# One core: convolution steps traced between matmul groups, 512-column weight blocks, tables behind the layer norm, small outputs in one store

## The chip, the cores and the metric

The kernel runs on one core of a Trainium2 chip. The metric is device time in microseconds (us): the median of three runs of the whole kernel. A profiled execution beside them gives the rows quoted here; its span is the time from its first to its last instruction.

## The reference

Two branches work on the layer norm of `A_q` and their outputs are added to it; the kernel computes the output and nine gradients, one for each differentiable input.

```python
def _A_ref(q, k, v, shift_k, ssm_k, ssm_D):          # S = 2048, D = 1024
    k_shift = sum(k_pad[:, t:t + S, :] * shift_k[:, ks - 1 - t] for t in range(ks))   # ks = 4 taps
    kv = k_shift * v
    y = irfft(rfft(kv, 2 * S) * rfft(ssm_k, 2 * S), 2 * S)[:S]      # long convolution per channel
    return q * (y + kv * ssm_D)

def _B_ref(x, W_gate, W_up, W_down):                 # F = 3584
    gate, up = x @ W_gate, x @ W_up
    return ((gate * (gate > 0)) * up) @ W_down

xn = layernorm(A_q)
out = A_q + _A_ref(xn, A_k, A_v, A_shift_k, A_ssm_k, A_ssm_D) + _B_ref(xn, B_W_gate, B_W_up, B_W_down)
# and the gradients of all ten inputs but B_x for grad_out
```

(The sums are written shorter here than in the original.)

## The kernel before

Everything is traced into one Tile program. A list scheduler orders each engine's instructions from the trace: among those that it estimates to be ready it takes the lowest rank, `tc.cur_priority`, which a helper class `Pri` sets. The queues of the engines are then fixed and in order; SyncE (SP) issues every DMA.

**The layer norm** (`layer_norm`, L465) takes 16 row tiles in batches of 1, 1, 2, 4, 4 and 4: two passes of ScalarE (ACT) per tile with an accumulated sum (L478, L485), a root per batch (L489), scalings on VectorE (DVE), a store of the normed rows to `xn_d`, and 8 transposes on TensorE (PE) into `xnT`. It has rank -10,000,000.

**The convolution branch** (`ABranch`) works on 8 groups of 128 channels with a table-driven Fourier transform of 8192 points, split into two matmul steps with a transposition (`flip`, two 32x32 stream transposes on VectorE) between them. `tables` (L101) computes the sine tables on ACT and VectorE. `loads` (L226) brings a group's six input tiles. `group` (L366) then runs in one go: the taps' row (`shift_b`), the transposed filter (`h_tile`), three forward transforms (`forward`: 8 matmuls of 512 columns, four ACT copies, `flip`, 32 matmuls of 128 columns, copies), the four taps on `k` (`taps`, L259, VectorE), three products of spectra (`cmul`), three inverse transforms (`inverse`, then `to_time` with 8 matmuls of 512 columns or `to_chan` with 32 of 64 columns), the gradients of `v`, `k` and of the taps (16 matmuls of 512 columns, `ps6`), and stores. The tap gradient `gsb` is stored element by element (4 x 128 values, L412), the gradient of `ssm_D` as one column of `ghn` (L421). Its matmuls and loads have rank 0 and up, its copies, VectorE work and stores 20,000,000 and up.

**The matmul branch** (`LnMlp`), rank 10,000,000 and up, has six stages: gate and up (`gate_up`, L511), hidden gradient (`grad_hidden`, L539), the gradient of the down weight (`grad_down`, L587), those of the gate and up weights (`grad_in`, L604), the output (`out_phase`, L636) and the input gradient (`grad_x`, L669). The first four walk the 3584 columns in 14 blocks of 256. `gate_up` writes the relu'd gate `rg`, the masked `up` and their product `ht` to DRAM; `grad_hidden` loads `rg` and `up` again, multiplies both with the hidden gradient and stores `gg_d` and `gu_d`. The pools: 16 row tiles (`act`) that hold in turn `xnT`, `goT`, `g_nat` and `xn_nat`; 5 weight blocks; 9 eviction tiles of 128 KB; 4 PSUM banks beside the 4 of the convolution.

So two rank ranges decide the order of the work: a convolution matmul goes ahead of any stage matmul as soon as the scheduler thinks it ready, and a convolution copy goes behind any eviction of the stages. The output stage needs the convolution's result `y_d`.

Of the kernel before, what the change touches and what calls it, by code (L numbers as in the profile page):

```python
# [11 lines left out]
BF16 = mybir.dt.bfloat16  # L12
F32 = mybir.dt.float32
# [4 lines left out]
P = 128  # L18
# [3 lines left out]
class Pri:  # L22


    def __init__(self, tc):
        self.tc = tc
        self.n = 0

    def at(self, base):
        self.n += 1  # L30
        self.tc.cur_priority = base + self.n


PR_LN = -10_000_000
PR_A_PE = 0
PR_A_LD = 0
PR_B = 10_000_000
PR_A_EV = 20_000_000
# [3 lines left out]
class ABranch:  # L42
# [18 lines left out]
    def mm(self, out, lhsT, rhs, start=True, stop=True):  # L61
        self.pri.at(PR_A_PE)
        self.nc.tensor.matmul(out, lhsT=lhsT, rhs=rhs, start=start, stop=stop)  # L63

    def act(self, out, in_):
        self.pri.at(PR_A_EV)
        self.nc.scalar.copy(out=out, in_=in_)

    def tt(self, out, in0, in1, op):
        self.pri.at(PR_A_EV)  # L70
        self.nc.vector.tensor_tensor(out=out, in0=in0, in1=in1, op=op)  # L71

    def vcopy(self, out, in_):
        self.pri.at(PR_A_EV)
        self.nc.vector.tensor_copy(out=out, in_=in_)

    def load(self, out, in_):
        self.pri.at(PR_A_LD)
        self.nc.sync.dma_start(out=out, in_=in_)

    def store(self, out, in_):
        self.pri.at(PR_A_EV)
        self.nc.sync.dma_start(out=out, in_=in_)

    def open(self):
        R = "right"
        self.con = self.pool("a_con", 1, side=R)
        self.lng = self.pool("a_lng", 2, side=R)
# [4 lines left out]
        self.tmp = self.pool("a_tmp", 2, side=R)  # L93
        self.sm = self.pool("a_sm", 2, side=R)
# [6 lines left out]
    def tables(self):  # L101
        nc, con, big, pri = self.nc, self.con, self.big, self.pri
        pri.at(PR_A_LD)
# [11 lines left out]
        self.skf = con.tile([P, self.NG, 4], F32, name="skf")  # L115
        negpi = con.tile([P, 1], F32, name="negpi")
# [109 lines left out]
    def loads(self, gi):  # L226
        nc, pri = self.nc, self.pri
        cg = slice(gi * P, (gi + 1) * P)
        S = self.S
        hn = self.ld.tile([P, 16, P], BF16, name="hn")  # L230
        self.load(hn[:].rearrange("p r c -> p (r c)"), self.ssm_k[cg, :])
        kp = self.lng.tile([P, 19, P], BF16, name="kp")
        pri.at(PR_A_LD)
# [6 lines left out]
        gt = self.ld.tile([P, 16, P], BF16, name="gt")  # L240
        self.load(gt[:], self.tview(self.g, cg))
        xt = self.ld.tile([P, 16, P], BF16, name="xt")
        self.load(xt[:], self.tview(self.xn_d, cg))
        return dict(gi=gi, cg=cg, hn=hn, kp=kp, vt=vt, gt=gt, xt=xt)

    def shift_b(self, st):
        gi = st["gi"]
        dg = self.sm.tile([P, 4, P], BF16, name="dg", bufs=1)
        for i in range(4):
            self.pri.at(PR_A_EV)  # L250
# [8 lines left out]
    def taps(self, st, out, src, offs):  # L259

        skb = st["skb"]
        for n, (i, off) in enumerate(offs):
            for hf in range(2):
                rows = slice(off + 8 * hf, off + 8 * hf + 8)
                sb = skb[:, i, :, :].to_broadcast([P, 8, P])
                o = out[:, 8 * hf:8 * hf + 8, :]
                if n == 0:
                    self.tt(o, src[:, rows, :], sb, ALU.mult)
                else:
                    t = self.tmp.tile([P, 16, P], BF16, name="tap", tag="tmp")  # L270
                    self.tt(t[:, 0:8, :], src[:, rows, :], sb, ALU.mult)
                    self.tt(o, o, t[:, 0:8, :], ALU.add)

    def h_tile(self, st):
# [4 lines left out]
        for r in range(16):  # L279
            self.pri.at(PR_A_PE)  # L280
# [4 lines left out]
    def flip(self, src):  # L285
# [4 lines left out]
        for c0 in range(0, 64, 32):  # L290
            self.pri.at(PR_A_EV)
# [3 lines left out]
    def forward(self, src, form_name, add_D=None):  # L295
# [10 lines left out]
        Bf = self.flip(B)  # L306
# [32 lines left out]
    def inverse(self, Q):  # L339
# [8 lines left out]
    def to_time(self, Cf, dst):  # L348
# [9 lines left out]
    def to_chan(self, Cf, dst):  # L358
# [7 lines left out]
    def group(self, st, nxt):  # L366
        nc, pri, gi, cg = self.nc, self.pri, st["gi"], st["cg"]
        kp, vt, gt, xt = st["kp"], st["vt"], st["gt"], st["xt"]
        self.shift_b(st)
        hT = self.h_tile(st)  # L370
        H = self.forward(hT, "H", add_D=self.sDb[:, cg].rearrange("p (o c) -> p o c", o=1))
        ksh = self.lng.tile([P, 16, P], BF16, name="ksh", bufs=1)
        self.taps(st, ksh, kp, [(3, 0), (2, 1), (1, 2), (0, 3)])
        kvt = self.ttile("kvt")
        self.tt(kvt[:, 0:16, :], ksh[:], vt[:], ALU.mult)
        K = self.forward(kvt, "K")
        self.tt(gt[:], gt[:], xt[:], ALU.mult)
        G = self.forward(gt, "G")
        if nxt is not None:
            st["next"] = self.loads(nxt)  # L380
        Y = self.cmul(H, K, False, "Y")
        GKV = self.cmul(H, G, True, "GKV")
        GH = self.cmul(K, G, True, "GH")

        yt = self.ttile("yt")
        self.to_time(self.inverse(Y), yt)
        self.store(self.tview(self.y_d, cg), yt[:, 0:16, :])

        gkv = self.ttile("gkv")
        self.to_time(self.inverse(GKV), gkv)  # L390
# [5 lines left out]
        pri.at(PR_A_EV)  # L396
        nc.gpsimd.memset(gks[:, 16:19, :], 0.0)
        self.store(gks[0:P - 1, 16:19, :], gks[1:P, 0:3, :])
        ps = self.ps.tile([P, 1024], F32, name="ps6", tag="aps")
        for i in range(4):  # L400
            pr = self.tmp.tile([P, 16, P], BF16, name="pr", tag="tmp")
            self.tt(pr[:], gks[:, 0:16, :], kp[:, 3 - i:19 - i, :], ALU.mult)
            for j in range(4):
                self.mm(ps[:, 0:512], self.hsel[:, i, :], pr[:, 4 * j:4 * j + 4, :].rearrange("p r c -> p (r c)"),
                        start=(i == 0 and j == 0), stop=(i == 3 and j == 3))
        gsf = self.sm.tile([4, P], F32, name="gsf", bufs=1)
        pri.at(PR_A_EV)
# [402 lines left out]
```

## Time and profile before

| | us |
|---|---|
| median of 3 runs | 2509.51 |
| lowest and highest run | 2496.64, 2514.35 |
| the profiled execution | 2500.66 |
| its span | 2498.9 |
| TensorE busy in the span | 2073.8 (83%) |
| VectorE busy | 1090.4 (44%) |
| ScalarE busy | 734.7 (29%) |
| GpSimd busy | 10.1 (0%) |

The busy shares are means over stages with different limits. The stages follow one another on TensorE: layer norm to about 62 us, gate and up from 81.7 to about 796, hidden gradient to about 1213, down weight to 1505.5, gate and up weights from there to 1904, output to 2103, input gradient to the end. The convolution lies beside the stages from gate and up to the down weight. A busy TensorE may still run at half speed: the granted clock of a stretch tells how much of it ran at 2.4 GHz (1.00) and how much at 1.2 GHz (0.50).

### The profile page before, as it was taken

How to read it: one execution, taken by the hardware profiler on the slowest of the kernel's cores; microseconds unless marked ns; L12 is line 12 of the kernel's file. 1: busy time of each engine (PE TensorE's matmuls, PEld its weight loads, DVE VectorE, ACT ScalarE, POOL GpSimd, SP SyncE). 2: the span in 40 equal slices, each digit the busy share in tenths (PEclk: the TensorE clock that was granted, in tenths of full speed). 3: DMA queues.
4: the chain of work that ended last, by engine and by line, in shares of the span. 5: the costliest groups of instructions: out<-in, count | busy, mean ns of one | idle time of the engine just before them, and what ended most of it. 6: DMA issues, size and time to landing. Idle time of an engine off the chain costs nothing. (4 is left out here: it accounts for less than half of the span.)

```text
span 2498.9 us, 36518 instructions
## 1 busy us (share of the span) xinstructions
PE 2073.8 (83%) x14931; PEld 1413.2 (57%) x15050; DVE 1090.4 (44%) x1778; ACT 734.7 (29%) x889; POOL 10.1 (0%) x30
## 2 busy tenths in 40 slices
PE   2784977868588657756778989999999999999998
PEld 1563756757466545544544437888886444444443
DVE  7784866868578257636757300000000221323323
ACT  9633545345363325335455311111110000000000
POOL 0000000000000000000000000000000000000000
PEclk9897989989899888988889999999999999999999
DMA  7347354463638787777852875343436995544542
GB/s 217 101 130 76 115 112 122 131 109 102 117 104 189 200 147 187 200 155 166 234 86 84 169 241 169 106 123 106 121 106 147 262 220 128 136 108 124 119 114 70
DMA packets 749993, 353.18 MB, mean 141 GB/s; under 512 B 422665, under 2 KB 721665, under 8 KB 749826
## 3 DMA queue, kind: packets, MB, share of 16 engines
q1 hardware_dynamic: 749826, 350.85, 58.4%
q8 instruction: 117, 1.92, 0.4%
q14 instruction: 50, 0.41, 0.1%
HBM read 154.93 MB, written 124.79 MB: 112 GB/s over the span
## 5 line engine op out<-in xcount | busy, mean ns | idle before, releaser
L525 PEld LDWEIGHTS <-xnT 128*128 128x128 bf16 x3584 | 351.9, 99 | 76.5 <-issue 23.8
L615 PEld LDWEIGHTS <-xn_nat 128*128 128x128 bf16 x3584 | 350.3, 98 | 48.7 <-DMA xn_nat<-xn_d 7.6
L559 PE MATMUL ps_h<-wdT,goT 128*128 128x256 bf16 x1792 | 227.9, 287 | 51.7 <-ACT gh L562 51.6
L664 DVE TENSOR_TENSOR o<-ps_o,ya 128x512 bf16<-128x512 f32 x32 | 21.4, 687 | 528.1 <-PE ps_o L662 528.1
L525 PE MATMUL ps_g<-wg,xnT 128*128 128x256 bf16 x1792 | 233.3, 277 | 0.1
L525 PE MATMUL ps_u<-wu,xnT 128*128 128x256 bf16 x1792 | 231.0, 276 | 0.2
L559 PEld LDWEIGHTS <-goT 128*128 128x128 bf16 x1792 | 182.6, 103 | 77.4 <-issue 45.6
L596 PE MATMUL ps_d<-g_nat,hs 128*128 128x512 bf16 x870 | 206.5, 389 | 19.2 <-DMA hs<-h_d 12.6
L615 PE MATMUL ps_w<-ggs,xn_nat 128*128 128x256 bf16 x1792 | 201.4, 274 | 4.1 <-DMA xn_nat<-xn_d 3.5
L662 PE MATMUL ps_o<-wd,hT 128*128 128x512 bf16 x878 | 194.6, 381 | 4.7 <-DMA hT<-h_d 3.7
L693 PE MATMUL ps_x<-wgT,ggT 128*128 128x512 bf16 x879 | 197.6, 379 | 0.9
L693 PE MATMUL ps_x<-wuT,guT 128*128 128x512 bf16 x877 | 197.3, 379 | 0.9
L615 PE MATMUL ps_w<-gus,xn_nat 128*128 128x256 bf16 x1792 | 197.9, 273 | 0.0
L618 ACT CAST wi<-ps_w 128x512 bf16<-128x512 f32 x112 | 65.5, 585 | 333.2 <-PE ps_w L615 333.2
L596 PEld LDWEIGHTS <-hs 128*128 128x128 bf16 x896 | 87.8, 100 | 125.1 <-issue 17.0
L662 PEld LDWEIGHTS <-hT 128*128 128x128 bf16 x896 | 87.8, 98 | 111.1 <-DMA hT<-h_d 5.0
L693 PEld LDWEIGHTS <-ggT 128*128 128x128 bf16 x896 | 87.6, 98 | 105.8
L693 PEld LDWEIGHTS <-guT 128*128 128x128 bf16 x896 | 87.6, 98 | 105.7
L63 PE MATMUL ps<-flp,FW 128*128 128x128 bf16 x768 | 58.7, 228 | 82.1 <-DVE flp L292 51.8
L562 ACT CAST gh<-ps_h 128x512 bf16<-128x512 f32 x112 | 66.1, 596 | 191.5 <-DMA gg_d<-upl 98.8
L695 DVE CUSTOM_DVE_ANT_0 gx<-ps_x,gy 128x512 f32<-128x512 f32 x32 | 22.1, 691 | 225.4 <-PE ps_x L693 214.7
L530 ACT ACTIVATE rg<-ps_g 128x512 bf16<-128x512 f32 x112 | 67.7, 605 | 170.3 <-PE ps_g L525 99.0
(165 smaller groups left out, 2110.9 us busy)
## 6 DMA issues: line engine op xcount, KB each, us to landing
rg_d<-rg SPq DMA_DIRECT2D x112, 128.0 KB
up_d<-up SPq DMA_DIRECT2D x112, 128.0 KB
h_d<-ht SPq DMA_DIRECT2D x112, 128.0 KB
rgl<-rg_d SPq DMA_DIRECT2D x112, 128.0 KB
upl<-up_d SPq DMA_DIRECT2D x112, 128.0 KB
gg_d<-upl SPq DMA_DIRECT2D x112, 128.0 KB
gu_d<-gh SPq DMA_DIRECT2D x112, 128.0 KB
hs<-h_d SPq DMA_DIRECT2D x28, 512.0 KB
```

What stands on the lines that cost most here:

```text
L63: self.nc.tensor.matmul(out, lhsT=lhsT, rhs=rhs, start=start, stop=stop)
L525: nc.tensor.matmul(ps[:, s * 256:s * 256 + 256], lhsT=xT[:, kt * P:(kt + 1) * P], rhs=w[:, kt, :], start=(kt == 0), stop=(kt == self.DT - 1))
L530: nc.scalar.activation(out=fl(rg), in_=pss[0][:], func=ACT.Relu)
L559: nc.tensor.matmul(ps[:, s * 256:s * 256 + 256], lhsT=xT[:, kt * P:(kt + 1) * P], rhs=w[:, kt, :], start=(kt == 0), stop=(kt == self.DT - 1))
L562: nc.scalar.copy(out=fl(gh), in_=ps[:])
L596: nc.tensor.matmul(ps[:], lhsT=hs(st)[:, j * P:(j + 1) * P], rhs=gn[st][:, ob * 512:ob * 512 + 512], start=(st == 0), stop=(st == self.ST ...
L615: nc.tensor.matmul(ps[:, d * 256:d * 256 + 256], lhsT=xn[st][:, dc * P:(dc + 1) * P], rhs=sl(st), start=(st == 0), stop=(st == self.ST - 1))
L618: nc.scalar.copy(out=wo[:].rearrange("p s f -> p (s f)"), in_=ps[:])
L662: nc.tensor.matmul(ps[:], lhsT=hT[:, kt, :], rhs=self.wd[:, kt, oc], start=(kt == 0), stop=(kt == self.FT - 1))
L664: nc.vector.tensor_tensor(out=o0[:, oc], in0=ps[:], in1=ya[:, oc], op=ALU.add)
L693: nc.tensor.matmul(ps[:], lhsT=T[:, kt, :], rhs=W[:, kt, oc], start=(i == 0), stop=(i == n - 1))
L695: V.tensor_tensor_reduce(out=gx[:, oc], in0=ps[:], in1=gy[:, oc], scale=1.0, scalar=0.0, op0=ALU.add, op1=ALU.add, accum_out=m[:, ob:ob + 1])
```

## The change

- **Ranks.** `Pri` has no ranges any more: `now()` advances a counter by 64 and gives it as rank, `late()` gives the same plus 100,000,000. Convolution matmuls and loads use `now()`, its copies, VectorE and GpSimd work and stores `late()`; the matmul stages call `now()` at every block and row tile. So ranks follow the order of tracing.
- **The order of tracing.** The stages `gate_up`, `grad_hidden`, `grad_down` and `grad_in` are generators that yield the nanoseconds of the matmuls just traced (3460 or 1730). `ABranch.steps` is a generator that yields how many nanoseconds shall pass until its next step. A loop runs the stages and, after the first 55,000 ns, draws a convolution step when the counted time has passed. The steps of a group are `group` cut into 17 pieces and reordered; a forward transform is cut into `fwd1` and `fwd2`, an inverse into `inv_a` and `inv_b`. When the convolution is through, `open_right` is called, inside the last of the four stages.
- **Blocks.** 512 columns instead of 256 in the four stages: one row tile by 512 columns per PSUM bank instead of two row tiles by 256. Weight tiles stay 512 KB, 6 instead of 5; evictions go to 5 tiles `e2` of 256 KB and 3 tiles `e1` of 128 KB. `rg` and `up` are the halves of one tile `ru`, loaded and stored in one DMA each; `gg_d` and `gu_d` become one array `ug_d`, written by one product of 128x1024 in which the hidden gradient is broadcast.
- **GpSimd.** `ht` and the multiplies of `taps` (without their adds) move from VectorE to GpSimd.
- **Tables.** `tables` is traced after the layer norm, and its ACT and VectorE instructions are ordered behind the layer norm's last ones (`issue_after`).
- **Loads.** `loads` is cut in two: `hn`, the gradient and the normed input (which are multiplied there) after the first spectrum of the previous group, `kp` and `vt` after its last tap product. `kp`, `vt` have one buffer each instead of two.
- **Small outputs.** `gsb` and the column of `ghn` are collected over the groups in `gs_all` and `gD_all`, transposed at the end (13 small transposes) and stored once each.

```diff
...
 class Pri:
+    LATE = 100_000_000
...
-    def at(self, base):
-        self.n += 1
-        self.tc.cur_priority = base + self.n
-
-
-PR_LN = -10_000_000
-PR_A_PE = 0
-PR_A_LD = 0
-PR_B = 10_000_000
-PR_A_EV = 20_000_000
+    def now(self):
+        self.n += 64
+        self.tc.cur_priority = self.n
+
+    def late(self):
+        self.n += 64
+        self.tc.cur_priority = self.n + self.LATE
...
     def taps(self, st, out, src, offs):
...
-                if n == 0:
-                    self.tt(o, src[:, rows, :], sb, ALU.mult)
-                else:
-                    t = self.tmp.tile([P, 16, P], BF16, name="tap", tag="tmp")
-                    self.tt(t[:, 0:8, :], src[:, rows, :], sb, ALU.mult)
-                    self.tt(o, o, t[:, 0:8, :], ALU.add)
+                t = o if n == 0 else self.tap.tile([P, 8, P], BF16, name="tap", tag="tap")[:]
+                self.pri.late()
+                self.nc.gpsimd.tensor_tensor(out=t, in0=src[:, rows, :], in1=skb[:, i, :, :].to_broadcast([P, 8, P]),
+                                             op=ALU.mult)
+                if n > 0:
+                    self.tt(o, o, t, ALU.add)
...
+    def steps(self):
+        nc, pri = self.nc, self.pri
+        nx = self.loads_1(0)
+        self.loads_2(nx)
+        for gi in range(self.NG):
+            st, nx = nx, None
+            cg, kp, vt, gt = st["cg"], st["kp"], st["vt"], st["gt"]
+            self.shift_b(st)
+            hT = self.h_tile(st)
+            ksh = self.lng.tile([P, 16, P], BF16, name="ksh")
+            self.taps(st, ksh, kp, [(3, 0), (2, 1), (1, 2), (0, 3)])
+            kvt = self.ttile("kvt")
+            self.tt(kvt[:, 0:16, :], ksh[:], vt[:], ALU.mult)
+            yield 7000
+            Hf = self.fwd1(hT)
+            yield 8000
+            Gf = self.fwd1(gt)
+            yield 8000
+            H = self.fwd2(Hf, "H", add_D=self.sDb[:, cg].rearrange("p (o c) -> p o c", o=1))
+            if gi + 1 < self.NG:
+                nx = self.loads_1(gi + 1)
+            yield 8000
+            Kf = self.fwd1(kvt)
+            yield 8000
+            G = self.fwd2(Gf, "G")
+            GKV = self.cmul(H, G, True, "GKV")
+            yield 8000
+            K = self.fwd2(Kf, "K")
+            Y = self.cmul(H, K, False, "Y")
+            yield 12000
+            Cg = self.inv_a(GKV)
+            yield 9000
+            Cy = self.inv_a(Y)
+            GH = self.cmul(K, G, True, "GH")
+            yield 8000
+            gkv = self.ttile("gkv")
+            self.inv_b(Cg, gkv)
+            gks = self.gradients(st, gkv, ksh)
+            yield 8000
+            yt = self.ttile("yt")
+            self.inv_b(Cy, yt)
+            self.store(self.tview(self.y_d, cg), yt[:, 0:16, :])
+            yield 8000
+            Ch = self.inv_a(GH)
+            yield 5000
+            ps = self.ps.tile([P, 1024], F32, name="ps6", tag="aps")
+            for i in range(4):
+                pr = self.tmp.tile([P, 16, P], BF16, name="pr", tag="tmp")
+                self.tt(pr[:], gks[:, 0:16, :], kp[:, 3 - i:19 - i, :], ALU.mult)
+                yield 3500
+                for j in range(4):
+                    self.mm(ps[:, 0:512], self.hsel[:, i, :], pr[:, 4 * j:4 * j + 4, :].rearrange("p r c -> p (r c)"),
+                            start=(i == 0 and j == 0), stop=(i == 3 and j == 3))
...
+            self.vcopy(self.gs_all[:, gi, :], gsf[:])
+            if nx is not None:
+                self.loads_2(nx)
+            ghn = self.ttile("ghn")
+            self.inv_b_chan(Ch, ghn)
+            ghf = ghn[:, 0:16, :].rearrange("p r c -> p (r c)")
+            self.vcopy(self.gD_all[:, gi:gi + 1], ghf[:, 0:1])
+            self.store(self.out_gh[cg, :], ghf)
+            yield 6000
+        self.small_outputs()
...
+    def gate_up(self, Wg, Wu, ru_d, h_d):
...
+                self.pri.now()
+                ps_g, ps_u = self.ps_tile("ps_g"), self.ps_tile("ps_u")
+                self.gemm8(ps_g, self.xnT[st], wg)
+                self.gemm8(ps_u, self.xnT[st], wu)
+                ru, ht = self.e2_tile("ru"), self.e1_tile("ht")
+                nc.scalar.activation(out=ru[:, 0, :], in_=ps_g[:], func=ACT.Relu)
+                nc.vector.scalar_tensor_tensor(out=ru[:, 1, :], in0=ru[:, 0, :], scalar=0.0, in1=ps_u[:],
+                                               op0=ALU.is_gt, op1=ALU.mult)
+                nc.gpsimd.tensor_tensor(out=ht[:], in0=ru[:, 0, :], in1=ru[:, 1, :], op=ALU.mult)
+                nc.sync.dma_start(out=ru_d[fb, st], in_=ru[:].rearrange("p a f -> p (a f)"))
+                nc.sync.dma_start(out=h_d[st * P:(st + 1) * P, cols], in_=ht[:])
+                yield 3460
...
+    def grad_hidden(self, Wd, g, ru_d, ug_d):
...
+                ru = self.e2_tile("rul")
+                nc.sync.dma_start(out=ru[:].rearrange("p a f -> p (a f)"), in_=ru_d[fb, st])
                 ps = self.ps_tile("ps_h")
...
+                self.gemm8(ps, goT[st], w)
+                gh = self.e1_tile("gh")
+                nc.scalar.copy(out=gh[:], in_=ps[:])
+                nc.vector.tensor_tensor(out=ru[:], in0=ru[:],
+                                        in1=gh[:].rearrange("p (o f) -> p o f", o=1).to_broadcast([P, 2, 512]),
+                                        op=ALU.mult)
+                nc.sync.dma_start(out=ug_d[st * P:(st + 1) * P, :, cols], in_=ru[:])
+                yield 1730
...
     b.layer_norm(x, xn_d, a.frm, "frm", a.tmp, "tmp", a.sm)
-    a.tables()
-    a.run()
-    a.close()
-    tc.cur_priority = PR_B
...
+    with tc.issue_after(b.ln_act.ins), tc.issue_after(b.ln_dve.ins):
+        a.tables()
...
+    a_steps, left = a.steps(), A_START
+    for ns in mlp():
+        left -= ns
+        while a_steps is not None and left <= 0:
+            d = next(a_steps, None)
+            if d is None:
+                a.close()
+                a_steps = None
+                b.open_right(B_W_down)
+            else:
+                left += d
     b.close_left()
...
```

## Rows read from the trace of the kernel before

**Rows 1.** Table of stretches: start:end, length, busy us (x count) per engine, clock, DMA.

```profile
62.00:796.00 734.00, 561.43 (x4973) 450.53 (x5003) 523.85 (x720) 335.45 (x365) 3.72 (x9) 0.91 0.52 116
796.00:1213.00 417.00, 277.27 (x2333) 220.59 (x2341) 237.56 (x404) 165.32 (x203) 1.23 (x3) 0.86 0.78 179
1213.00:1505.50 292.50, 246.37 (x1296) 117.13 (x1322) 125.90 (x149) 110.18 (x124) 0.83 (x2) 0.92 0.64 156
1505.50:1519.50 14.00, 9.99 (x61) 5.57 (x59) 0.00 (x0) 0.58 (x1) 0.00 (x0) 0.88 0.95 323
...
1904.00:2103.00 199.00, 194.35 (x881) 87.92 (x898) 39.16 (x59) 0.58 (x1) 0.00 (x0) 0.99 0.92 214
2103.00:2498.90 395.90, 385.40 (x1759) 175.29 (x1793) 118.12 (x273) 0.00 (x0) 0.00 (x0) 0.99 0.46 113
```

**Rows 2.** Chain of work that ended last, in order of time: start us, us, what.

```profile
1361.80 0.45 PE ps L63 x8
...
1392.66 1.11 PE ps L63 x32
...
1519.54 384.88 PE ps_w L615 x3524
...
2103.51 1.08 PE ps_x L693 x5
...
2482.35 7.95 PE ps_x L693 x36
```

**Rows 3.** Waits: engine, line, waited for, us in total, times, longest us.

```profile
PE ps L63 <- DVE flp L292: 116.5, 47, 17.1
...
PE ps L63 <- DVE hT L75: 59.4, 7, 22.9
...
PE ps_sk L63 <- ACT ghn L67: 33.9, 7, 8.4
...
PE pst L281 <- ACT ghn L67: 22.9, 7, 3.9
...
PE ps_h L559 <- ACT gh L562: 51.6, 21, 12.4
...
ACT gh L562 <- DMA gg_d<-upl: 98.8, 22, 16.3
...
DVE tap L71 <- DMA gks<-gks: 49.6, 8, 19.4
...
DVE hT L75 <- DMA out_dram<-ghn: 31.4, 2, 23.1
```

**Rows 4.** Groups of instructions of ACT and DVE: count, busy us, mean ns, idle before.

```profile
L292 DVE STREAM_TRANSPOSE flp<-B 128x1024 f32<-128x1024 f32 x48 | 89.6, 1911 | 37.5 <-ACT B L67 37.4
...
L67 ACT CAST B<-ps 128x1024 bf16<-128x1024 f32 x96 | 92.7, 1026 | 80.8 <-remote 73.4 <-PE ps L63 4.5 <-PE ps_u L525 2.6
...
L67 ACT CAST ghn<-ps 128x1024 bf16<-128x1024 f32 x16 | 72.7, 4787 | 36.5 <-PE ps L63 19.3 <-DMA out_dram<-gv 17.3
...
L533 DVE TENSOR_TENSOR ht<-rg,up 128x512 bf16<-128x512 bf16 x112 | 46.7, 417 | 1.4
...
L71 DVE TENSOR_TENSOR tap<-kp,skb 128x1024 bf16<-128x1024 bf16 x48 | 31.6, 682 | 0.1
```

**Rows 5.** The same view, POOL (GpSimd) alone.

```profile
L397 POOL MEMSET gks<- 128x384 bf16 x8 | 3.3, 417 | 1282.2 <-DMA y_d<-yt 710.8 <-DVE upl L563 223.7 <-DVE gv L71 206.7
...
masks.py:199 POOL TENSOR_SCALAR_AFFINE_SELECT identA<-identA 128x128 bf16<-128x128 bf16 x1 | 0.3, 282 | 0.0
```

**Rows 6.** Timeline: start us, us, engine, line, instruction, count, idle before.

```profile
15.12 1.28 ACT L489 ACT_TABLE_LOAD   x1
...
54.73 1.04 ACT L478 ACTIVATE ln_j<-ln_x 128x1024 bf16<-128x1024 bf16 x1
...
58.54 1.90 PE L281 MATMUL pst<-identA,hn 128*128 128x128 bf16 x16
...
81.72 1.91 PE L525 MATMUL ps_g<-wg,xnT 128*128 128x256 bf16 x16
```

## What the rows let one forecast

> **What bounds the kernel now.** I read the stages first, then the waits, then single instructions. The table of stretches [rows 1] shows two kernels in one. In the last two stretches TensorE (PE) has work all the time: they take 199 and 396 us with 194 and 385 us of PE busy, at a granted clock of 0.99; the long matmul run from 1519.54 us on is as dense [rows 2]. From 62 to 1505 us it is not so: three stretches of 734, 417 and 292.5 us hold 561, 277 and 246 us of PE busy, so PE is idle for 358 us, and the mean granted clock is 0.91, 0.86 and 0.92. A mean of 0.90 over 1443 us means that about 300 us ran at the lower of the two levels, 1.2 instead of 2.4 GHz. No other engine is full there: VectorE (DVE) works 887 of these 1443 us, ScalarE (ACT) 611.
>
> The waits name the cause [rows 3]. PE's queue is in order, and the convolution's matmuls stand in it directly behind what feeds them: 116.5 us for the transposed half-products `flp` (47 times, 2.5 us each), 59.4 us for `hT`, 33.9 and 22.9 us for ACT's copy `ghn`; 233 us in these four rows. The hidden-gradient stage has a wait of its own: 51.6 us for the eviction `gh`, itself late because its buffers wait for the stores of `gg_d` (98.8 us). Before all that, the first gate matmul starts only at 81.72 us [rows 6]. So three things are to be had: the idle PE, the half clock around it, and the start.
>
> **The unit prices of PE work.** A 512-column matmul: 32 groups of 56 run from 2103.51 to 2490.30 us [rows 2], 386.79/1792 = 215.8 ns. A 256-column one: 384.88/3524 = 109.2 ns [rows 2], so two make 218.4 ns. The 512-column blocks save 2.6 ns on each of 4480 pairs (gate, up, hidden, two weight gradients), 12 us; the weight loads that they halve were hidden already. 128-column matmuls take 0.45/8 = 56 ns, 64-column ones 1.11/32 = 35 ns [rows 2], the 16 transposes of a group 1.90 us [rows 6].
>
> **The sum.** I build the new span from its parts, since nearly all of it should be PE work.
>
> *Four matmul stages*: 5376 matmuls of 512 columns, 1160 us. *Convolution*: per channel group 57 matmuls of 512 columns (12.3 us), 192 of 128 (10.8), 32 of 64 (1.1) and the transposes (1.9), 26.1 us, times 8 = 209 us. By the distances written into the trace, 117 us of stage matmuls per group after the first 55, it ends at 991 of the 1160 us. *Last two stages*: untouched but for the layout of `ug_d`, 199 + 396 = 595 us [rows 1].
>
> *Start*: 45 us. Today the sine tables are mixed into the layer norm on ACT, and each switch loads a function table for 1.28 us [rows 6]. Behind the layer norm, ACT has 32 passes of 1.04 us and six function loads of 1.28 us for the root [rows 6], 41 us; with the first input's arrival and the last tile's hand-overs I estimate 50. The convolution's first matmuls no longer stand ahead of the gate stage, whose first group needs only one layer-norm tile and one weight block. I credit 5 us of it under the layer norm. Ends: 30 us (much of the first block hidden) and 82 us (no gain). The moved tables have the first 55 us of the gate stage as cover; if that cover is gone, the ACT time saved here is paid there, which the upper end holds.
>
> *Stage changes*: 24 us. The 16 row tiles are still reloaded into the same buffers; `xn_nat` leaves 14 us between 1505.5 and 1519.5 [rows 1], and I add 5 us for each of the other two changes. Ends 10 and 40.
>
> *Waits of the convolution on PE*: the point of the change. Each of its 17 PE pieces per group (136 in all) is traced with 3.5 to 12 us of other matmuls before the next, and producer and consumer mostly stand two pieces apart. Behind one matmul step come at most four copies of 1.03 us and two transposes of 1.9 us [rows 4], 8 us without queueing; but behind the last piece ACT's two `ghn` copies take 9.6 us [rows 4] against 6 us of cover. So most waits fall under the cover, the `ghn` one in part. I keep a quarter of 233 us, 58 us; ends 0 and 233. Clock: if PE was busy in half of the 300 slow us (it is in three quarters of all), they cost 75 us; a quarter is 19 us; ends 0 and 75.
>
> *Hidden stage*: 30 us. Each step of 1.73 us now loads 256 KB in one transfer and stores 256 KB, with five buffers where nine small ones served three steps. The stage moves 59 MB so, 11.5 MB of transposed loads and some 8 MB of the convolution, in 193 + 1.7 × 26 = 237 us: 330 GB/s. The highest rate in the rows is 323 GB/s, in the 14 us from 1505.5 on [rows 1]; the stage itself ran at 179. So DMA is as full as PE there. Ends 5 (at 323 GB/s) and 80 (at 250 GB/s, halfway between the rows).
>
> *Fewer transfers*: 434 loads and stores fall away, but the queue engine (SP) does not bind, so no term. The 16 stores of `gsb` and of one column of `ghn` move into one pair at the end. A store of `ghn` held `hT` back for up to 23.1 us (31.4 us in all, [rows 3]), which is inside the 233. The 13 small transposes and three copies that replace them run beside the weight-gradient stage and nothing waits for them: nothing, or 5 us if that cover is gone.
>
> *GpSimd*: 128 tap multiplies of 128x1024 and 112 products `ht` leave VectorE (0.68 and 0.42 us each, [rows 4]; 134 us in all). What one costs on GpSimd no row shows. Below, VectorE's 0.68 us; above, twice the select's rate, for two inputs. The select reads and writes 128 columns in 282 ns [rows 5], 2.2 ns a column, 2.3 us for 1024; the memset writes 384 in 417 ns, 1.1 us for 1024. I take 2.3 us, because the select reads a tensor as the multiply does: 128 × 2.3 + 112 × 1.15 = 420 us out of some 1300, so GpSimd is no bound, nor at 4.6 us. The wait that this adds: the taps on `gks` wait for a copy by DMA (49.6 us, up to 19.4, [rows 3]); behind them on GpSimd now stand the `ht` products of the gate stage, and behind those its five `ru` buffers, 5 × 3.46 = 17 us of cover, then PE. Moved loads: `kp` and `vt` have one buffer instead of two and are loaded behind the last product that reads them; the next group's taps want them at once, its third transform 31 us later, which is their cover.
>
> Sum: 1160 + 209 + 595 + 45 + 24 + 58 + 19 + 30 = 2140 us of span against 2498.9; 1.8 us lie around the span in the profiled execution (2500.66), which is inside the three runs and 9 us under their median. I predict 2140 us.
>
> **A rule that speaks against the change.** The select's row gives 2.3 us for a multiply and tells nothing of VectorE meanwhile [rows 5]. The Trainium skill's page "GPSIMD Engine Reference", sections "Performance versus the Vector engine" and "When to use GPSIMD", advises against elementwise work with two inputs on GpSimd, at about 2.6 cycles an element (2.2 us here at its 1.2 GHz, an estimate from that page), and says that it shares its SBUF interfaces with VectorE. By the speed alone the sum stays; by the sharing it becomes the second rival.
>
> **Rivals.** *All waits hidden*: the cover is enough everywhere, the terms of 58, 19 and 30 us go: 2033 us. For it speaks that no engine is full, against it the `ghn` copies.
>
> *VectorE held up by GpSimd*: VectorE keeps 887 − 134 − 18 = 735 us (the 18: one 128x1024 multiply for two of 0.42 us, 112 times in the hidden stage). If it stood still whenever GpSimd works, it would need 735 + 420 = 1155 of some 1300 us, and less would be free in the hidden stage, where 68 steps of 0.68 us stand in each group's 143 us beside some 73 us of its own. Half of the waits (117) and of the clock's price (37) then stay, and the hidden stage gives its 80: 2033 + 234 = 2267 us. Nothing in this trace has both engines at tensor work, so it can't be excluded.
>
> *The pacing does nothing*: the order on PE comes from a scheduler's estimates; if it places the matmuls as tightly as now, 233 and 75 us stay, and 60 in the hidden stage: 2401 us. Against it: the matmuls now carry rank in trace order, so one that is ready is no longer pulled forward.
>
> *Slower*: each convolution matmul stands at a set place of an in-order queue, and its copies have the lowest rank on ACT and VectorE. If they come behind several evictions each time, PE waits at each of the 136 pieces. The span exceeds the old one when the mean wait exceeds (2499 − 2033)/136 = 3.4 us, against 2.5 us of today's `flp` waits; at 4 us it is 2577 us. For it: today's waits reach 17.1 and 22.9 us [rows 3]. Against it: ACT and VectorE are free for a third of the time or more [rows 1].
>
> **How the numbers follow.** Forecast 0.54 (its own range 2070 to 2220), all hidden 0.13, VectorE held up 0.17, pacing without effect 0.09, slower 0.07. The range 2030 to 2320 reaches over the first three and leaves out the 0.16 of the last two. A measurement here tells about 1% from no change; over 1% faster are the first three and most of the fourth, 0.88; within 1% 0.05; slower 0.07.
>
> **What would show it.** Right: the first gate matmul before 50 us; waits of PE on `flp`, `hT` and `ghn` under 80 us together; a granted clock over 0.97 in every stretch; the convolution's last store some 170 us before the output stage. Wrong: PE waiting for evictions in the hidden stage with DMA near 300 GB/s (that term too small); 128x1024 multiplies of VectorE well over 0.68 us while GpSimd runs (second rival); waits of PE as long as now (third, fourth); a late `ht` with PE behind it (GpSimd's queue).

## The result and the profile after

The changed kernel takes 2411.17 us, median of 4 runs (2409.23 to 2413.66), against 2506.85 us of the kernel before in the same runs: a ratio of 0.962, 95% interval 0.958 to 0.966. It is 3.8% faster, but 271 us above the forecast and 91 us above the range. The profiled execution took 2409.23 us, its span is 2407.4 us.

The table of stretches (start:end, length, busy us and count per engine, clock, DMA share, GB/s): gate and up, hidden gradient, down weight, two pieces of the gate and up weights, output, input gradient.

```profile
57.40:641.60 584.20, 490.64 (x2589) 234.01 (x2638) 383.14 (x410) 233.18 (x270) 250.02 (x159) 0.94 0.42 125
641.60:968.70 327.10, 245.32 (x1235) 115.74 (x1258) 207.24 (x223) 129.75 (x166) 73.23 (x34) 0.89 0.78 227
968.70:1313.00 344.30, 281.75 (x1589) 137.74 (x1620) 223.19 (x216) 176.59 (x191) 78.44 (x37) 0.91 0.38 111
1313.00:1550.00 237.00, 195.45 (x1072) 94.11 (x1092) 125.47 (x118) 96.14 (x106) 57.42 (x26) 0.94 0.37 113
1550.00:1811.60 261.60, 247.54 (x1138) 112.15 (x1161) 5.26 (x10) 46.99 (x74) 0.00 (x0) 0.99 0.47 150
1811.60:2012.30 200.70, 193.09 (x880) 87.38 (x896) 39.44 (x59) 0.58 (x1) 0.00 (x0) 1.00 0.92 213
2012.30:2407.40 395.10, 385.17 (x1758) 175.26 (x1792) 118.10 (x273) 0.00 (x0) 0.00 (x0) 0.99 0.47 113
```

Compare [rows 1]. The last two stretches are within 1 us of what they were, 595.8 us. Where the convolution runs (57.4 to 1550) the clock is still 0.89 to 0.94 and PE is idle for 279 us, or some 23 us less: of 6608 weight loads there, 123 have no record of their matmul. Behind it PE is nearly full. Much of the loss was moved, not removed. The waits say where to (engine, line, waited for, us in total, times, longest us):

```profile
DVE gk L72 <- POOL tap L278: 117.0, 25, 13.5
...
POOL tap L278 <- DMA gks<-gks: 70.8, 6, 26.9
...
PE ps_u L585 <- DVE ru L601: 69.3, 21, 8.7
DVE ksh L72 <- POOL tap L278: 64.9, 19, 15.3
...
PE ps L64 <- DVE flp L301: 30.3, 11, 8.7
PE ps_sk L64 <- ACT ghn L68: 25.0, 3, 21.2
...
PE ps L64 <- DVE hT L76: 13.8, 3, 7.7
```

PE's waits for `flp`, `ghn` and `hT` shrank from 233 us [rows 3] to 78 (with the 8.8 us for which the transposes `pst` wait for `ghn`). In their place stands a new one: PE waits 69.3 us for the masks `ru` on VectorE, and VectorE waits 182 us for the taps on GpSimd. The groups of instructions (count, busy us, mean ns, idle before) show that the instructions themselves changed:

```profile
L301 DVE STREAM_TRANSPOSE flp<-C 128x1024 f32<-128x1024 f32 x48 | 89.0, 1914 | 1.3 <-ACT C L68 1.0
L72 DVE TENSOR_TENSOR ksh<-ksh,tap 128x1024 bf16<-128x1024 bf16 x48 | 78.0, 1656 | 64.9 <-POOL tap L278 64.9
L601 DVE SCALAR_TENSOR_TENSOR ru<-ru,ps_u 128x512 bf16<-128x512 bf16 x112 | 75.2, 679 | 86.7 <-PE ps_u L585 55.1 <-issue 20.9 <-ACT ru L600 4.7
L72 DVE TENSOR_TENSOR gk<-gk,tap 128x1024 bf16<-128x1024 bf16 x48 | 74.2, 1568 | 117.0 <-POOL tap L278 117.0
...
L278 POOL TENSOR_TENSOR tap<-kp,skb 128x1024 bf16<-128x1024 bf16 x48 | 110.1, 2313 | 8.8 <-DVE ksh L72 8.8
```

GpSimd takes 2.3 us for a tap, as forecast. But an add of 128x1024 on VectorE, an instruction the size of the taps that took 0.68 us [rows 4], now takes 1.57 to 1.66 us in the mean. The masks `ru`, which read PSUM, and the transposes `flp` kept their time (679 ns and 1.9 us). A timeline of one group's taps (start us, us, engine, line, instruction, count, idle before):

```profile
259.68 4.20 POOL L278 TENSOR_TENSOR tap<-gks,skb 128x1024 bf16<-128x1024 bf16 x2 [6.41 <-issue]
...
261.84 3.19 DVE L72 TENSOR_TENSOR gk<-gk,tap 128x1024 bf16<-128x1024 bf16 x2 [10.36 <-POOL tap L278]
...
264.50 4.57 POOL L278 TENSOR_TENSOR tap<-gks,skb 128x1024 bf16<-128x1024 bf16 x2 [0.63 <-DVE gk L72]
267.03 2.59 DVE L72 TENSOR_TENSOR gk<-gk,tap 128x1024 bf16<-128x1024 bf16 x1 [2.01 <-POOL tap L278]
269.54 0.67 DVE L601 SCALAR_TENSOR_TENSOR ru<-ru,ps_u 128x512 bf16<-128x512 bf16 x1
...
270.27 3.57 PE L585 MATMUL ps_u<-wu,xnT 128*128 128x512 bf16 x8 [8.60 <-DVE ru L601]
```

The adds wait for the taps and, beside them, run slowly; the mask stands in VectorE's queue behind an add of 2.59 us and that add's wait of 2.01 us for its tap; PE waits 8.60 us for the bank that the mask frees. So two things can cost time here: instructions that last longer, and an in-order queue that waits for a late tap.

### The profile page after: what moved, and what is told of

Read it like the earlier page. It is cut to its first block, busy times and chain, and to the rows that moved or that the text cites. A ratio compares the mean times of both kernels' runs of the same rounds, so it can differ in the third digit from the quotient of the medians.

```text
span 2407.4 us, 26357 instructions
## 1 busy us (share of the span) xinstructions
PE 2053.3 (85%) x10379; PEld 969.4 (40%) x10583; DVE 1136.8 (47%) x1445; ACT 722.2 (30%) x880; POOL 463.1 (19%) x270
## 2 busy tenths in 40 slices
DMA packets 591166, 352.52 MB, mean 146 GB/s; under 512 B 410817, under 2 KB 530625, under 8 KB 591042
## 4 chain that ended last, share of the span: by engine, by line
PE 38%; DVE 8%; DMA 6%; SPq 3%; issue 2%; ACT 2%; POOL 2%; DVEq 0%; ACTq 0%; POOLq 0%
PE ps_x L775 16%; PE ps_w L659 11%; PE ps_o L742 6%; PE ps_d L659 3%; DMA ugs<-ug_d 2%; DVE t L72 2%; DVE flp L301 2%; POOL tap L278 2%; PE ps L64 1%; SPq L734 1%; DVE ksh L72 1%; DVE Y L72 1%; DMA hs<-h_d 1%; ACT G L68 1%; DMA gks<-gks 1%
## 5 line engine op out<-in xcount | busy, mean ns | idle before, releaser
L659 PE MATMUL ps_w<-ugs,xn_nat 128*128 128x512 bf16 x1752 | 401.1, 383 | 20.9 <-DMA ugs<-ug_d 16.5
L585 PE MATMUL ps_u<-wu,xnT 128*128 128x512 bf16 x881 | 230.8, 402 | 82.6 <-DVE ru L601 69.3
L585 PEld LDWEIGHTS <-xnT 128*128 128x128 bf16 x1792 | 177.5, 101 | 300.2 <-issue 115.7
L659 PEld LDWEIGHTS <-xn_nat 128*128 128x128 bf16 x1792 | 175.3, 99 | 233.6 <-issue 34.4
L585 PE MATMUL ps_h<-wdT,goT 128*128 128x512 bf16 x872 | 212.4, 396 | 16.8 <-DVE ru L601 9.9
L585 PE MATMUL ps_g<-wg,xnT 128*128 128x512 bf16 x865 | 220.2, 386 | 2.4 <-ACT ru L600 0.5
L603 POOL TENSOR_TENSOR ht<-ru 128x512 bf16<-128x512 bf16 x112 | 151.6, 1358 | 364.0 <-DVE ru L601 274.8
L585 PEld LDWEIGHTS <-goT 128*128 128x128 bf16 x896 | 89.9, 101 | 147.1 <-issue 54.8
L633 DVE TENSOR_TENSOR rul<-rul,gh 128x1024 bf16<-128x1024 bf16 x112 | 94.7, 857 | 90.6 <-DMA rul<-ru_d 61.8
L72 DVE TENSOR_TENSOR gk<-gk,tap 128x1024 bf16<-128x1024 bf16 x48 | 74.2, 1568 | 117.0 <-POOL tap L278 117.0
```

The lines of the kernel that those rows point to most:

```text
L585: self.nc.tensor.matmul(ps[:], lhsT=xT[:, kt * P:(kt + 1) * P], rhs=w(kt), start=(kt == 0), stop=(kt == self.DT - 1))
L603: nc.gpsimd.tensor_tensor(out=ht[:], in0=ru[:, 0, :], in1=ru[:, 1, :], op=ALU.mult)
L633: nc.vector.tensor_tensor(out=ru[:], in0=ru[:], in1=gh[:].rearrange("p (o f) -> p o f", o=1).to_broadcast([P, 2, 512]), op=ALU.mult)
L659: self.nc.tensor.matmul(ps[:], lhsT=lhsT(st), rhs=rhs(st), start=(st == 0), stop=(st == self.ST - 1))
```

## The experiments

The kernel before took 2495.76 to 2530.89 us in the different sets of runs. Where kernels of different sets are compared, their ratios to it are used. Three theories stood at the start: GpSimd's work holds VectorE up; the pacing is worth little; the gain of other parts is only smaller than forecast.

**GpSimd undone.** Each part alone, then both:

```diff
-                self.nc.gpsimd.tensor_tensor(out=t, in0=src[:, rows, :], ...
+                self.nc.vector.tensor_tensor(out=t, in0=src[:, rows, :], ...      # e1, e3
...
-                nc.gpsimd.tensor_tensor(out=ht[:], ...
+                nc.vector.tensor_tensor(out=ht[:], ...                            # e2, e3
```

> The tap multiplies go back to VectorE; the products ht stay on GpSimd. Theory 'VectorE held up by GpSimd': the adds behind the taps last 0.68 us again instead of 1.6 us, VectorE's 182 us of waiting for taps go, and with them most of PE's 69 us behind the masks ru and half of its other waits: about 2300 us (2260 to 2350). Rival 'VectorE is simply full': 88 us more work on it makes the kernel slower than 2411 us. Rival 'the pacing does nothing': PE's waits stay, 2411 us within 25.

> The products ht go back to VectorE; the tap multiplies stay on GpSimd. Theory 'held up', with the taps as the part that hurts: 47 us more on VectorE, the waits for taps stay: 2411 us within 30. If ht beside VectorE's own work is what hurts, as much as e1 gains should come here instead: under 2350 us.

> No tensor work on GpSimd: taps and ht on VectorE as before the change, all else as after it. Theory 'held up': 2270 to 2350 us, PE idle between the first gate matmul and the end of the convolution under 160 us instead of 279. Rival 'VectorE is full': above 2411 us. Rival 'the pacing does nothing': 2411 us within 25.

Measured: 2253.16 us with the taps on VectorE (ratio 0.902, 0.900 to 0.904), 2383.93 with `ht` there (0.954, 0.951 to 0.957), 2230.82 with both (0.892, 0.890 to 0.895). By the ratios the GpSimd part costs 175 us (0.962 against 0.892), 151 to 155 by the taps and 20 to 24 by `ht`; e3 lies below the range expected of it. The kernel without it beats both kernels. One of its groups of instructions:

```profile
L72 DVE TENSOR_TENSOR gk<-gk,tap 128x1024 bf16<-128x1024 bf16 x48 | 31.7, 683 | 0.1
```

The busy times on its page, and on that of the changed kernel:

```profile
PE 2025.7 (91%) x10583; PEld 958.2 (43%) x10583; DVE 1087.8 (49%) x1685; ACT 720.9 (32%) x880; POOL 10.2 (0%) x30
```

```profile
PE 2053.3 (85%) x10379; PEld 969.4 (40%) x10583; DVE 1136.8 (47%) x1445; ACT 722.2 (30%) x880; POOL 463.1 (19%) x270
```

Without work on GpSimd VectorE does 240 instructions more and is busy 49 us less. What was taken off it came back as longer instructions.

**Contention or late results?** The last kernel (taps and `ht` on VectorE), with 128 copies of the tap multiplies on GpSimd on half the partitions, whose result nobody reads:

```diff
                 self.nc.vector.tensor_tensor(out=t, in0=src[:, rows, :], in1=skb[...], op=ALU.mult)
+                self.nc.gpsimd.tensor_tensor(out=self.gs_all[64:P], in0=src[64:P, rows, :], in1=skb[64:P, ...], op=ALU.mult)
```

> e3 (all tensor work on VectorE) plus, beside each of the 128 tap multiplies, an idle copy of it on GpSimd, on half of the partitions, whose result nobody reads. GpSimd's work is back, but no instruction of another engine waits for its result. If the price of the taps on GpSimd is the standstill of VectorE's instructions with two SBUF inputs alone, this is near the kernel with the taps on GpSimd, 2340 to 2385 us. If it is VectorE's in-order waiting for the taps alone, it stays at 2231 us within 25. In between, both have a part; 2290 us is expected.

2398.28 us (0.954, 0.953 to 0.956). Its tables of groups and waits:

```profile
L72 DVE TENSOR_TENSOR gk<-gk,tap 128x1024 bf16<-128x1024 bf16 x48 | 63.1, 1335 | 0.1
...
L281 POOL TENSOR_TENSOR gs_all<-gks,skb 64x1024 bf16<-64x1024 bf16 x64 | 156.8, 2450 | 521.0 <-DVE gks L72 432.5 <-DMA gks<-gks 84.7
```

```profile
PE ps_u L588 <- DVE ru L604: 62.3, 20, 10.1
```

No other engine waits for these results, and still 165 us are lost against the kernel of the same runs with mixed tables (2233.70 us, below), 155 by the ratios against the kernel without GpSimd work. The add takes 1.34 us instead of 0.68 and PE's wait for `ru` is back (9.3 us without the dummies). So contention alone is enough for a loss of this size.

It does not follow that contention makes up the whole price in the changed kernel. The busy times of the kernel with the dummies, and of the one with the taps alone on GpSimd (e2), with half of its adds:

```profile
PE 2059.4 (86%) x10583; PEld 967.0 (40%) x10583; DVE 1318.8 (55%) x1685; ACT 721.3 (30%) x880; POOL 321.7 (13%) x158
```

```profile
PE 2071.2 (87%) x10583; PEld 970.1 (41%) x10583; DVE 1145.9 (48%) x1557; ACT 722.2 (30%) x880; POOL 312.3 (13%) x158
```

```profile
L72 DVE TENSOR_TENSOR gk<-gk,tap 128x1024 bf16<-128x1024 bf16 x48 | 71.8, 1517 | 100.4 <-POOL tap L278 100.4
```

With the dummies VectorE's own multiplies lengthen too, and its instructions take 231 us more in all. With the taps on GpSimd they take some 145 us more (1145.9 against 1087.8 less 128 multiplies of 0.68), and VectorE waits 160 us for taps besides, 100 of them before the adds shown. If the loss went with the lengthening alone, contention would be about 100 of the 155 us of the taps: an estimate from these rows. No run separates the two shares; the price of the late taps stays open.

**The order of tracing undone**, with GpSimd and without: the convolution traced first, in the old rank ranges. The new order of the steps inside a group stays.

```diff
+    pri.base, pri.n = 0, 0
     ... a.tables()
+    for _ in a.steps():
+        pass
+    a.close()
+    pri.base, pri.n = 10_000_000, 0
...
-    a_steps, left = a.steps(), A_START      # and the loop that draws steps
+    for _ in mlp():
+        pass
```

> All of the change but its order: the convolution is traced whole before the four stages and has the three rank ranges of the kernel before (its matmuls and loads ahead of the stages, its copies behind them). If the pacing is worth something, this is slower than the changed kernel: 2480 us or more. If the pacing does nothing, 2411 us within 25.

> Blocks, merged transfers, loads, small outputs and tables of the change, but the order and ranks of the kernel before and no tensor work on GpSimd: what is left is neither pacing nor GpSimd. If the two add up as e3 and e4 suggest (180 and 106 us), about 2335 us. If the pacing only shows its worth where GpSimd delays VectorE, this is near e3, 2231 to 2260 us. If blocks and transfers bring nothing by themselves, it is near the kernel before, 2495 us.

2517.32 us with GpSimd (1.008, 1.005 to 1.011) and 2328.18 without (0.926, 0.925 to 0.927). By the ratios the pacing is worth 116 us with GpSimd (1.008 against 0.962) and 84 without (0.926 against 0.892): it works. And GpSimd costs more in the old order, 206 us against 175. PE's wait for `flp` holds about half of that, 171.4 us with GpSimd and 71.2 without:

```profile
PE ps L66 <- DVE flp L303: 171.4, 31, 15.3
```

```profile
PE ps L66 <- DVE flp L303: 71.2, 31, 6.5
```

That left a question: without GpSimd and without pacing the kernel was still 7% faster than before, and no term of the forecast had such a size.

**Tables, distances, `ghn`.** Four single edits of the kernel without GpSimd work: the tables free to mix with the layer norm; `ghn` copied by VectorE; the distances times 1.12 and times 0.75.

```diff
-    with tc.issue_after(b.ln_act.ins), tc.issue_after(b.ln_dve.ins):      # e7
-        a.tables()
+    a.tables()
...
-            self.act(dv[:, n0:n0 + 16, :], ps[:])                          # e8
+            self.vcopy(dv[:, n0:n0 + 16, :], ps[:])
...
-                left += d
+                left += d * 1.12                                           # e11; 0.75 in e12
```

> e3 with the sine tables free to mix with the layer norm again. If the tables behind the layer norm matter as forecast, the first gate matmul comes 10 us or more later than at 57.7 us and the time is 10 to 25 us above e3. If the start is bound by something else, 2231 us within 10.

> e3 with the two copies ghn of each group on VectorE instead of ScalarE, where one takes 4.8 us. PE's waits for ghn in e3 are 34 us. If they are paid in full and VectorE copies at its 1.2 us, 2195 to 2210 us; if VectorE needs as long for the strided write as ScalarE, no gain or a loss.

> The kernel without tensor work on GpSimd (2230.8 us), every distance between convolution steps times 1.12, so that the convolution ends near 1110 instead of 991 of the 1160 us of counted stage matmuls. It still has 145 us of idle PE between the first gate matmul and the output stage. If short distances cause them: 2205 to 2220 us. If they have other causes (transfers, engines that are late whatever the distance): 2231 us within 8.

> The same kernel with every distance times 0.75, so that the convolution ends near 757 of the 1160 counted us, in the down-weight stage. If the distances are what hides the waits: 2260 to 2330 us, with longer waits of PE for flp, ghn and hT. If the order alone does it (matmuls in trace order, a scheduler that places them): 2231 us within 15.

2233.70 us (0.888, 0.887 to 0.889), 2227.30 (0.886, 0.884 to 0.887), 2249.67 (0.890, 0.887 to 0.893), 2301.13 (0.910, 0.907 to 0.913). With mixed tables the first gate matmul starts at 65.95 us instead of 57.7, and nothing of it is left at the end. `ghn` on VectorE gains 1% at most; one such copy takes 4.63 us there in the median, about as long as on ACT (4.79 us in the mean, [rows 4]). Wider distances change nothing that these runs can tell, closer ones cost 2%: the distances do hide waits, and those of the change are wide enough.

**The small outputs undone** in the kernel without GpSimd work: the stores of `gsb` and of `ghn`'s column element by element in each group (e9), or of the column alone (e13); and the other way round, the small outputs alone in the kernel before (e10, where `gs_all` is kept on 4 rows at each of partitions 0, 32, 64 and 96 to save space).

```diff
-            self.vcopy(self.gs_all[:, gi, :], gsf[:])                                  # e9
...
+            self.vcopy(gsb[:], gsf[:])
+            self.store(self.out_gsk[cg, :].rearrange("c i -> i c"), gsb[:])
...
-            self.vcopy(self.gD_all[:, gi:gi + 1], ghf[:, 0:1])                         # e9, e13
             self.store(self.out_gh[cg, :], ghf)
+            self.store(self.out_gsD[cg].rearrange("(p o) -> p o", o=1), ghf[:, 0:1])
```

> The kernel without tensor work on GpSimd (2230.8 us), with the small outputs stored again group by group. In the kernel before, hT waited 31.4 us in all for stores of ghn and PE 59.4 us for hT. If that carries over: 2255 to 2270 us and PE waits for hT of 20 us or more. If the looser order hides those stores: 2231 us within 10.

> The kernel before with one part of the change alone: gsb and the column of ghn are collected on the chip and stored once at the end; order, blocks, tables and engines stay as before. If the element stores hold up all transfers for some 20 us in each of the 8 groups whatever the order: 2300 to 2360 us, a ratio of 0.92 to 0.94, and PE waits for hT and for the eviction gh well under the 59.4 and 51.6 us of before. If what they cost was only the 31.4 us of hT: 2460 to 2500 us, 0.98 to 1.00.

> The kernel without tensor work on GpSimd (0.892 of before) with only the column of ghn stored element by element again, 128 of the 640 elements per group; gsb stays collected. With both undone it was 0.961. If the cost goes by the element: a fifth of it, a ratio of 0.90 to 0.91. If each such store holds the queues by itself: 0.92 to 0.94. If only the stores of gsb, whose elements lie 8 bytes apart in DRAM, are costly: 0.885 to 0.897.

e9: 2432.98 us (0.961, 0.959 to 0.964), some 8% more than without the edit (0.892), beyond both expectations. e10, in the old order: 2383.90 us (0.942, 0.940 to 0.944): this part alone gives the old kernel 147 us, more than the whole change gave. e13: 2322.08 us (0.918, 0.915 to 0.922). The column, a fifth of the elements, makes 0.026 of the 0.069 lost in e9: more than a cost by the element would give it, and just under the range for a cost by the store.

The timeline of e9 around the first such store:

```profile
270.51 0.56 SPq L84 DMA_DIRECT2D out_dram<-gsb  x1
274.33 2.20 SPq L84 DMA_DIRECT2D out_dram<-ghn  x1
...
279.85 12.54 SPq L606 DMA_DIRECT2D h_d<-ht  x1
...
313.39 0.60 ACT L601 ACTIVATE ru<-ps_g 128x512 bf16<-128x512 f32 x1 [21.95 <-DMA ru_d<-ru]
313.56 0.42 DVE L604 TENSOR_TENSOR ht<-ru 128x512 bf16<-128x512 bf16 x1 [25.05 <-DMA h_d<-ht]
...
319.90 2.72 PE L586 MATMUL ps_u<-wu,xnT 128*128 128x512 bf16 x6 [22.61 <-DVE ru L602]
```

It is not one transfer that is late. SP takes 12.54 us to issue one store of `h_d` (1.15 us at most in the kernel without the edit), stores of the gate stage that have nothing to do with the small outputs don't land, the eviction buffers stay taken, ACT and VectorE stand still for 22 and 25 us, then PE for 22.61 us. The stretch of 30 us behind it, in e9, in the kernel without the edit, and in the kernel before (its last column is GB/s):

```profile
280.00:310.00 30.00, 17.27 (x80) 7.61 (x78) 8.51 (x14) 5.46 (x7) 0.00 (x0) 0.88 0.83 39
```

```profile
280.00:310.00 30.00, 29.41 (x147) 13.46 (x145) 25.66 (x37) 11.84 (x16) 0.00 (x0) 1.00 0.46 141
```

```profile
195.00:225.00 30.00, 8.17 (x65) 6.91 (x64) 7.30 (x13) 3.75 (x4) 0.00 (x0) 0.61 1.11 41
```

All traffic together falls from 141 to 39 GB/s; it falls first, to 7 and 15 GB/s from 280 to 290 us, while PE is still busy. The kernel before shows much the same, 41 GB/s behind its first group, with PE busy 8 of 30 us. In e10 PE's waits became these:

```profile
PE ps L63 <- DVE flp L295: 103.6, 47, 5.2
...
PE ps_h L583 <- ACT gh L586: 29.9, 18, 3.6
...
PE ps L63 <- DVE hT L75: 8.8, 4, 4.0
```

`hT` fell from 59.4 to 8.8 us, `gh` from 51.6 to 29.9 and the longest `flp` wait from 17.1 to 5.2 [rows 3], though the `flp` row keeps 103.6 of its 116.5 us: rows that I had read as causes of their own had one partly in common. Part of what stood under "waits of the convolution" was no matter of order at all.

## Why the forecast was wrong

**The ledger.** Going from kernel to kernel by their ratios: before 1; small outputs alone 0.942; with blocks, loads and tables 0.926; with the pacing 0.892; with GpSimd 0.962. Of 2507 us these steps are −145, −41, −84 and +175 us, −95 together. The second also holds the new order inside a group and whatever the blocks and small outputs do to each other.

**The span by the forecast's own terms.** 2407.4 = 57.4 (start) + 1754.2 (to the output stage's first matmul at 1811.6) + 595.8. The forecast had 45 + 1500 + 595: 1369 of work and 131 for stage changes, waits, clock and hidden stage. So 254 us of the miss lie in the middle and 12 at the start. Without work on GpSimd the middle takes 1575.3 us (57.7 to 1633.0): 179 of the 254 are GpSimd, 75 are not.

**The step that failed: GpSimd costed at nothing.** The price of a multiply was right (2.3 us; 463 us busy against 420), and the sum asked only whether GpSimd itself binds. What it does to VectorE stood in the second rival, at 2267 us and 0.17. The rival's mechanism, VectorE held up while GpSimd works, is one that e6 shows; its price, 127 us, was too small against 175, and the wait of VectorE's queue for late taps, 182 us in the trace, was not in it. It spread a standstill over a mean and gave back half of the waits. The trace shows bursts instead: the taps of a group come together, and in them the masks that free PE's banks stand behind adds of up to four times their old length (1.6 us in the median, 2.94 at most) and behind the waits for taps. Each us of GpSimd's work on taps costs about half a us (153 for 303 in e2, 165 for 311 in e6), each on `ht` a seventh (22 for 156 in e1). A likely reason is that `ht` runs between the masks, which don't suffer, and little else stands there; no run tests it.

The Trainium skill's page "GPSIMD Engine Reference", section "Specifications", limits the contention to VectorE instructions in a 2-port mode or with two SBUF inputs. The trace agrees for two SBUF inputs: the 128x1024 adds went from 0.68 to between 1.57 and 1.66 us in the mean, the masks with one input in PSUM stayed at 679 ns, and `flp`, with one input, at 1.9 us. No run isolates the 2-port mode.

**The second step that failed: "fewer transfers ... no term".** I counted queue entries and one wait of 31.4 us [rows 3]. The row that mattered was the rate: 41 GB/s in the 30 us behind the first group's store, inside a stretch whose mean of 116 [rows 1] hides it. That is a gain of about 145 us that the sum had no name for. Since the sum was built up from the work of the new kernel, the missing name did not move the total; it gave the credit to the pacing, which was to cover these "waits". The gain of the pacing itself, 84 to 116 us, is smaller than the 175 of waits, 56 of clock and 30 of hidden stage that I gave to the order of work.

The page "DMA: Bandwidth & Descriptors" of the Trainium skill, section "Specifications", gives 512 bytes as the least transfer for full rate, with read-modify-write below. The trace agrees that 2-byte elements are costly: behind the first such stores in e9 the traffic of all transfers is down to 39 GB/s for 30 us.

**Step by step, the rest.** *Start*: 57.4 instead of 45 us, inside the ends. ACT's last root ended at 52 us, and from there to the first gate matmul it took another 5; I had counted 50 for both, and the credit of 5 for the convolution's matmuls was not to be had. Tables behind the layer norm bring 8 us of first matmul, nothing at the end. *Waits of the convolution*: 78 us in the named rows, under the 80 given as the sign; right, but PE's 69.3 us for `ru` is not among them. *Hidden stage*: 327 us against 237 + 30; without GpSimd 290.7, so 54 us over the 237. The reason given, DMA as full as PE, is not what PE waits for. The rate is 227 and 256 GB/s there, under the 323 seen elsewhere, though DMA's busy share of 0.88 is higher there than in the other stages beside the convolution. And of PE's 45 us of waits in the kernel without GpSimd about 40 are for the convolution's results, above all `ghn` (12.4) and `gsf` (9.3), and under 6 for evictions. The stage in its table of stretches, and the waits in it:

```profile
553.80:844.50 290.70, 239.62 (x1259) 114.36 (x1258) 181.82 (x254) 129.21 (x166) 1.24 (x3) 0.92 0.88 256
```

```profile
PE ps_sk L64 <- ACT ghn L68: 12.4, 1, 12.4
PE ps L64 <- DVE gsf L434: 9.3, 2, 5.5
```

*Clock*: 0.89 to 0.94 where over 0.97 was the sign; without GpSimd 0.99 in the gate stage and 0.92 in the hidden one. *Work and last stages*: the 595 us were right to 1 us. *Pacing does nothing* fell with e4 and e5, *slower* with the result itself, *all waits hidden* with the 206 us that stay in the middle without GpSimd. 145 of them are idle PE, in many small waits, no row of them over 16 us; the other 61 are PE busy for longer than the 1369 us counted, which the clock under 1.00 can explain in part. What keeps the clock down was not separated.

## What to carry to other kernels

Before work moves to an idle GpSimd, list the VectorE instructions with two SBUF inputs that will run beside it, who stands behind them in VectorE's queue, and who will wait there for GpSimd's results; whether GpSimd itself is full is not the whole question. Look at DMA in slices of some 10 us, not in means over a stage: a hole in the rate that begins at a store of single elements, while transfers are issued, tells more than the waits that it causes, which show up under other names all over the trace. Collect such outputs on the chip.

## What the runs showed of the hardware

A store of 2-byte elements slows nearly all transfers in flight. In e13, with 128 elements alone, the traffic of the last 10 us of this stretch is all but gone; below it the same 10 us of the kernel without the edit, where SP issued the same stores about 1 us earlier:

```profile
280.00:285.00 5.00, 4.95 (x24) 2.25 (x23) 5.00 (x9) 0.73 (x2) 0.00 (x0) 1.00 2.54 110
285.00:290.00 5.00, 4.98 (x23) 2.14 (x22) 5.00 (x10) 2.39 (x3) 0.00 (x0) 1.00 1.00 6
290.00:295.00 5.00, 4.95 (x24) 2.25 (x23) 1.06 (x2) 0.00 (x0) 0.00 (x0) 1.00 0.07 2
```

```profile
285.00:290.00 5.00, 4.98 (x24) 2.14 (x22) 5.00 (x10) 4.09 (x5) 0.00 (x0) 1.00 0.30 105
290.00:295.00 5.00, 5.00 (x24) 2.23 (x23) 5.00 (x4) 0.76 (x2) 0.00 (x0) 1.00 0.62 154
```

6 and 2 GB/s for 10 us against 105 and 154, with a busy share of 2.54 before it. A share over 1 suggests that a packet's time is counted where it begins; then packets begun there lasted far beyond their slice. Short packets as such don't seem to do it: the changed kernel moves 410,817 packets of under 512 bytes, and where its rate falls to 0 GB/s, from 265 to 270 us, SP had issued nothing since 255.03. Why 2-byte stores do, and why the column costs more per element than `gsb` (by the difference of e9 and e13), stays open.

GpSimd's time goes by columns: its multiply of 64x1024 took 2.42 to 2.45 us in the mean, the taps of 128x1024 2.30 to 2.31. And a GpSimd that works on partitions 64 to 127 alone slows VectorE's instructions over all 128 (the add from 0.68 to 1.34 us).
